# Two moves in a fused attention and gated-MLP kernel: half of the first query weights' loads to another engine's queue, two blocks of gate logits to an earlier stage

## The chip, the cores and the metric

The kernel runs on one core of a Trainium2 chip. The metric is the device time of one execution in microseconds (us), and a kernel's time is the median of several executions. A core has a matrix engine (TensorE, PE in the profile), a vector engine (VectorE, DVE), an engine for activations (ScalarE, ACT), GpSimd (POOL) and SyncE (SP), which here does nothing but issue DMA transfers. Every engine carries out its own instructions in a fixed order, and waits at an instruction until the semaphores that it names have been raised by other engines or by a transfer that has landed. Matrix products accumulate in PSUM, a small memory of eight banks of 128 x 512 fp32 elements; everything else lies in the on-chip SBUF (128 partitions) or in HBM.

## What is computed

The input x has S = 2048 rows of D = 1024 bf16 elements. Two branches are computed from it and are mixed by a gate for each row:

```python
g = _sigmoid((x * gate_w).sum(-1, keepdims=True))
# branch A: q, k, v = x @ wqkv, 32 heads of 32; each row attends to W = 8 rows,
# its own and those 2, 4, ... 14 rows before it; softmax; then @ wo
# branch B: gelu(x @ w_gate) * (x @ w_up) @ w_down, inner size 3584
return g * a + (1 - g) * b
```

## The kernel before

**Tiling.** The rows are handled in four chunks, c = 0 to 3, of 512 rows each, and two chunks form a pair. The weights stream through SBUF for each pair. All large products use a seven-product form of a 2 x 2 block product (Strassen's), so they need sums and differences of blocks, called forms here: of x (`x_forms`, lines L516 to L521, results T1 to T4), of the query, key and value weights (`qkv_forms`, L709), and of the down and output weights (`down_forms`, L1266). The forms are made on VectorE.

**Stages of a pair.** For each pair, `qkv_pair` computes queries, keys and values. Its first part, `first_pair`, begins with products of plain blocks (L592), whose weights need no forms, copies each finished bank to a second one as a start value (L602, L604), and goes on with products that need forms (L772; their results are read by L625, L637, L657, L667 and, for keys and values, L808 to L847). The `ffn` stage follows (L1136), with the gate and up products of branch B. `down` (L1305) multiplies by w_down and wo, and mixes the branches when banks are read (L1346, L1377, L1383): its `steps` are pairs (m, g), where m from 1 to 6 is one of the seven products and g a half of the chunk's rows. `main` (L1396) sets this order: chunks 0 and 1, then `down(0)`, then `qkv_pair(2)`, and so on.

**The gate.** `gate(c)` (L866) computes the logits x * gate_w of a chunk as products with the column of gate weights on TensorE (L874, eight matmuls for a chunk) into a bank; VectorE transposes the bank into a tile `zt` (L880), after which the bank is free, and copies 16 columns of it to `zq` (L884). `gate_sum` adds them up later (L898, L903). For chunks 0 and 1, `gate` is called inside `first_pair`; for 2 and 3, from `main` between the end of `down(0)` and `qkv_pair(2)`. The tile `zt` lies in one of two buffers with the tag `u2`; two other buffers have the tag `m5`. The down stage uses both tags as well.

**Attention.** Scores are made on VectorE: q times shifted k (L937) and sums over head parts (L943). The result is turned by a DMA transpose (L1006), softmaxed, spread by ScalarE (L1066), turned back by two DMA transposes (L1075), and multiplied with shifted v (L1084, 1.22 us each), which is summed (L1094, L1098, L1102). Every L1084 of a half chunk waits for the second L1075. All this work runs beside TensorE's stages, and the attention of chunk 1 is still going on when `down(0)` and `qkv_pair(2)` run.

**What sets the order.** A class `Weave` (L44) merges several streams of operations (`main`, `loads`, `x_forms`, `qkv_forms`, `attention`, `scores` and others) into one order for each engine. It always emits the operation with the smallest planned start plus a bias, where planned costs and due times are written into the code. Banks are handed out by `bank_take` to the earliest planned release. The chip then executes each engine's order as it stands. So moving one operation in `main` can reorder the others on VectorE and SyncE.

**Loads.** Nearly all loads are issued by SyncE in order, into 20 slots of a ring. At the start, SyncE issues two loads of query weights (L428, 512 KB each: blocks kt 0 to 1 and 2 to 3), a transposing load of half of chunk 0 (L357, in `early_x`), two more L428 (kt 4 to 5, 6 to 7), two L357 for chunk 1, and the key weights (L352). ScalarE issues one load of x rows (L312) and `gate_w` (L318), and then loads its activation table (L325). The other half of chunk 0 comes in as plain rows and is transposed by TensorE (L550), copied out by L559 and L561.

Of the kernel before, what the change touches and what calls it, by code (L numbers as in the profile page):

```python
# [11 lines left out]
F32 = mybir.dt.float32  # L12
AP = bass.AP

P = 128
# [4 lines left out]
SC = 512  # L20
# [134 lines left out]
def kernel(  # L155
# [12 lines left out]
    nc = tc.nc  # L168
    Bsz, S, D = A_x.shape
# [4 lines left out]
    KT = D // P  # L174
    KH = KT // 2
# [56 lines left out]
    n = NWIN * AC  # L232
# [83 lines left out]
    load_rows(nc.scalar, 2, 0)  # L316
    grow = xbuf[0:KT, 1, 0:P]
    nc.scalar.dma_start(out=grow, in_=gate_w.rearrange("(k p) -> k p", p=P))  # L318
    warm = xbuf[:, 0, 0:2]
    nc.vector.memset(warm, 0.0)  # L320
    for i, n_ in enumerate([SC] * 8):
# [15 lines left out]
    w.pipe = 3.2  # L337

    vbuf = hrow[:, 0:KT, :]
    qbuf = hrow[:, KT:2 * KT, :]  # L340
    NPREP = FH + NTH
    NSTG = 3
    def stage(i):
# [3 lines left out]
    def qkv_src(which, k0, n):  # L347
        return A_wqkv[k0 * P:(k0 + n) * P, which * D:(which + 1) * D].rearrange("(k p) n -> p k n", p=P)
# [75 lines left out]
    def loads():  # L424
        for kt in range(0, KT, 2):
            if kt == KH:
                yield from early_x(0)
            o = Op("SP", (2 * P * D * 2, 0.7), lambda kt=kt: nc.sync.dma_start(  # L428
                out=qbuf[:, kt:kt + 2], in_=qkv_src(0, kt, 2)), key=("wqkv", 0, 0, kt))
            yield o  # L430
            w.done["wqkv", 0, 0, kt + 1] = o
        yield from early_x(1)
        yield from load_qkv(0, 1)
        yield Op("SP", (KT * P * D * 2, 1.0), lambda: [nc.sync.dma_start(out=vbuf[:, hf * KH:(hf + 1) * KH],
                                                                        in_=qkv_src(2, hf * KH, KH)) for hf in range(2)],
                 key=("wqkv", 0, 2))
        yield load_prep(0)
        yield load_prep(2)
        yield from load_block(0, 0)
        yield load_prep(4)  # L440
        yield from load_block(0, 1)
        for b in range(2, NBLK):
            yield from load_block(0, b)
            if 4 + 2 * (b - 1) < NPREP:
                yield load_prep(4 + 2 * (b - 1))
        for sup in range(NSUP):
            c0 = 2 * sup
            more = sup + 1 < NSUP
            if more:
                yield from load_down(c0)  # L450
                for n in range(3):
                    yield from load_qkv(c0 + 2, QVK[n], range(KT) if n == 0 else [k for i in range(KH) for k in (i, i + KH)],
                                        [("wq", c0 + 2, QVK[n - 1], 3, KH - 1)] if n else [])
                for b in range(NE // FB):
                    yield from load_block(sup + 1, b, [("wq", c0 + 2, QVK[2], 3, KH - 1)])
                yield from load_down(c0 + 1)
                for b in range(NE // FB, NBLK):
                    yield from load_block(sup + 1, b)
            else:
                yield from load_down(c0)  # L460
                yield from load_down(c0 + 1)
# [404 lines left out]
    def gate(c):  # L866
        i, free = bank_take()
        dx = [("x", c, kt) for kt in range(KT)] if c else []

        def go():  # L870
            for r in range(KT // 4):
                for q in range(4):
                    kt = 4 * r + q
                    nc.tensor.matmul(banks[i][32 * q:32 * (q + 1), :], lhsT=gcol[:, kt:kt + 1].to_broadcast([P, 32]),  # L874
                                     rhs=xT(c, kt), start=(r == 0), stop=(r == KT // 4 - 1),
                                     tile_position=(0, 32 * q), skip_group_check=True)
        o = pe(KT // 4 + 1, go, ([free] if free else []) + dx + [("gcol",)], key=("z", c))
        yield o
        zt = work.tile([P, SC], F32, tag="u2", bufs=2, name="zt")
        e = dve(0.63, lambda: nc.vector.transpose(out=zt[:], in_=banks[i][:]), [o], bias=-2.0 if c < 2 else None)  # L880
        yield e
        bank_give(i, e)
        zq = small.tile([P, SC // 32], F32, tag="zq", bufs=2, name="zq")
        e = dve(0.1, lambda: nc.vector.tensor_copy(out=zq[:], in_=zt[:].rearrange("p (b j) -> p b j", j=32)[:, :, 0]), [e],  # L884
                key=("zq", c))
        yield e
        zc = small.tile([P, NST], F32, tag="zc", bufs=2, name="zc")
        ez = small.tile([P, NST], F32, tag="ez", bufs=2, name="ez")
        omg = small.tile([P, NST], F32, tag="omg", bufs=3, name="omg")
        gates[c] = (ez, omg, zq, zc)  # L890
# [439 lines left out]
    def down_rest(c, prod, ev, A, Bk, Dk, m5, u2, omg, steps):  # L1330
        s0 = c * SC
        last = c == NCH - 1
        eng = nc.sync if last else nc.gpsimd

        def evac(e_op, j, nh, ost):
            yield e_op
            yield Op("SP" if last else "POOL", (P * NW * 2, 0.5),
                     lambda: eng.dma_start(out=o2[s0 + j * P:s0 + (j + 1) * P, nh * NW:(nh + 1) * NW], in_=ost[0]),  # L1338
                     [e_op])

        def ost_tile(box):
            box.append(work.tile([P, 2 * SC], BF16, tag="gl", bufs=3, name="ost")[:, 0:NW])
            return box[0]

        def scaled(bk, om, dst):
            return nc.scalar.activation(out=dst, in_=banks[bk][:], func=ACT.Copy, scale=om)  # L1346

        for m, g in steps:
            if True:
                j1, j2 = 2 * g, 2 * g + 1  # L1350
                om1, om2 = omg[:, j1:j1 + 1], omg[:, j2:j2 + 1]
                box = []
                if m == 1:
                    o = yield from prod(A[g], m, g, False, [ev[g, "seed"]])
                    e = act(0.6, lambda g=g, om1=om1, box=box: scaled(A[g], om1, ost_tile(box)), [o, ("omg", c)])
                    yield from evac(e, j1, 0, box)
                    bank_give(A[g], e)
                elif m == 2:
                    Dk[g], fr = bank_take()
                    o = yield from prod(Dk[g], m, g, True, [fr])  # L1360

                    def cp(g=g, om2=om2):
                        m5[g] = work.tile([P, NW], F32, tag="m5", bufs=2, name="m5d")
                        scaled(Dk[g], om2, m5[g][:])
                    ev[g, "m5"] = act(0.6, cp, [o, ("omg", c)])
                    yield ev[g, "m5"]
                elif m == 3:
                    o = yield from prod(Bk[g], m, g, False, [ev[g, "seed"]])

                    def cp2(g=g, om1=om1):  # L1370
                        u2[g] = work.tile([P, NW], F32, tag="u2", bufs=2, name="u2d")
                        scaled(Bk[g], om1, u2[g][:])
                    ev[g, "u2"] = act(0.6, cp2, [o])
                    yield ev[g, "u2"]
                elif m == 4:
                    o = yield from prod(Bk[g], m, g, False, [ev[g, "u2"]])
                    ev[g, "x"] = dve(0.67, lambda g=g, om2=om2, box=box: nc.vector.scalar_tensor_tensor(  # L1377
                        out=ost_tile(box), in0=banks[Bk[g]][:], scalar=om2, in1=m5[g][:], op0=ALU.mult, op1=ALU.add),
                        [o, ev[g, "m5"]])
                    yield from evac(ev[g, "x"], j2, 1, box)  # L1380
                elif m == 5:
                    o = yield from prod(Dk[g], m, g, False, [ev[g, "m5"]])
                    e = dve(0.67, lambda g=g, om1=om1, box=box: nc.vector.scalar_tensor_tensor(  # L1383
                        out=ost_tile(box), in0=banks[Dk[g]][:], scalar=om1, in1=u2[g][:], op0=ALU.mult, op1=ALU.add),
                        [o, ev[g, "u2"]])
                    yield from evac(e, j1, 1, box)
                    bank_give(Dk[g], e)
                else:
                    o = yield from prod(Bk[g], m, g, False, [ev[g, "x"]])
                    e = act(0.6, lambda g=g, om2=om2, box=box: scaled(Bk[g], om2, ost_tile(box)), [o])  # L1390
                    yield from evac(e, j2, 0, box)
                    bank_give(Bk[g], e)
        if steps[-1][0] == 6:
            w.done[("down", c)] = o

    def main():  # L1396
# [8 lines left out]
        yield from ffn(0, 0, FT, parts)  # L1405
        yield from parts[2]
        yield from halo(2)
        yield from gate(2)
        yield from gate(3)
        yield from qkv_pair(2, [0])  # L1410
        yield from qkv_pair(2, [2, 1])
        yield from gate_sum(2)
# [43 lines left out]
```

## Time and profile before

Four executions took 725.27 to 726.68 us, with a median of 725.85.

| | before |
|---|---|
| median of 4 | 725.85 us |
| the profiled execution, its own time | 726.68 us |
| its span in the profile | 724.9 us |
| TensorE busy | 711.8 us (98%) |
| VectorE busy | 610.4 us (84%) |
| ScalarE busy | 323.9 us (45%) |
| GpSimd busy | 73.8 us (10%) |
| moved by DMA | 176.84 MB |

The profile is of one execution. Times in it count from the start of the span; an engine is busy while it carries out an instruction, and the time between two instructions of an engine is put down to whatever ended it: a semaphore of another engine, a transfer, or only its own issue. In the order of time, `qkv_pair(0)` begins at about 6 us, `down(0)` ends at 308.4 us and `qkv_pair(2)` follows it. A line number such as L880 is one of the program above.

### The profile page before, as it was taken

What the parts mean: (1) busy time and instruction counts of PE and PEld (TensorE: products, weight loads), DVE (VectorE), ACT (ScalarE), POOL (GpSimd) and SP (SyncE); (2) the same over time, 40 slices, a digit from 0 to 9 for tenths busy, and PEclk for the clock granted to TensorE, in tenths of its full rate; (3) what the DMA queues carried; (4) which work ended last, traced back from release to release, by engine and by line L of the source; (5) the groups of instructions that cost most, each with busy time, mean ns of one, the idle gap of its engine ahead of it and who ended that gap; (6) DMA issues with size and microseconds to landing.
All of it is one profiled execution on the core that took longest, in us unless ns stands there. A gap on an engine that the chain in (4) does not pass through costs nothing.

```text
span 724.9 us, 9885 instructions
## 1 busy us (share of the span) xinstructions
PE 711.8 (98%) x3337; PEld 343.1 (47%) x3337; DVE 610.4 (84%) x862; ACT 323.9 (45%) x547; POOL 73.8 (10%) x130
## 2 busy tenths in 40 slices
PE   7999999999999999979999999999999999999997
PEld 4556544444444444445655444444444444444443
DVE  4989999999999989799779998799999997849300
ACT  3354585555585522144465413257556755310110
POOL 0020333343121000100000000100000000001000
PEclk9999999999999999999999999999999999999999
DMA  9953899996897799932468899997657755999892
GB/s 255 365 193 95 251 293 312 368 312 213 184 264 217 244 231 339 345 127 81 148 181 283 263 316 329 321 318 188 176 152 183 181 155 165 304 308 375 295 335 96
DMA packets 184179, 176.84 MB, mean 244 GB/s; under 512 B 58304, under 2 KB 140224, under 8 KB 184000
## 3 DMA queue, kind: packets, MB, share of 16 engines
q1 hardware_dynamic: 174512, 145.53, 68.7%
q0 software_dynamic: 9328, 30.42, 11.6%
q8 instruction: 26, 0.43, 0.2%
q10 hardware_dynamic: 288, 0.26, 0.1%
q14 instruction: 25, 0.20, 0.1%
HBM read 132.12 MB, written 31.46 MB: 226 GB/s over the span
## 4 chain that ended last, share of the span: by engine, by line
PE 93%; DMA 3%; DVE 2%; SPq 1%; issue 0%; ACT 0%; DVEq 0%
PE ps L1136 47%; PE ps L1305 27%; PE ps L772 18%; DMA ring<-in_A_wqkv_dram 2%; DVE ring L709 1%; DMA ring<-dforms 1%; PE ps L592 1%; SPq L357 1%; DMA hT<-in_A_wqkv_dram 1%; DVE zt L880 0%; SPq L428 0%; DVE lend L520 0%; DVE tf L521 0%; DVE tf L518 0%; DVE lend L837 0%
## 5 line engine op out<-in xcount | busy, mean ns | idle before, releaser
L1136 PEld LDWEIGHTS <-ring 128*128 128x128 bf16 x1568 | 153.3, 98 | 185.0 <-issue 0.5
L1136 PE MATMUL ps<-lend,ring 128*128 128x512 bf16 x896 | 212.6, 379 | 0.0
L1136 PE MATMUL ps<-tf,ring 128*128 128x512 bf16 x672 | 164.3, 379 | 0.0
L1305 PE MATMUL ps<-ring,hT 128*128 128x512 bf16 x708 | 160.6, 379 | 0.0
L1305 PEld LDWEIGHTS <-hT 128*128 128x128 bf16 x708 | 69.3, 98 | 83.5
L1084 DVE TENSOR_TENSOR xbuf<-xbuf,lend 128x2048 bf16<-128x2048 bf16 x64 | 77.6, 1218 | 14.2 <-DMA xbuf<-xbuf 14.1
L772 PEld LDWEIGHTS <-ring 128*128 128x128 bf16 x512 | 64.8, 127 | 48.8 <-issue 2.5
L937 DVE TENSOR_TENSOR xbuf<-qo,lend 128x2048 bf16<-128x2048 bf16 x64 | 77.3, 1218 | 2.7 <-ACT lend L830 2.6
L943 DVE TENSOR_TENSOR xbuf<-xbuf 128x2048 bf16<-128x2048 bf16 x56 | 68.2, 1218 | 0.2
L772 PE MATMUL ps<-tf,ring 128*128 128x512 bf16 x256 | 58.4, 379 | 2.4 <-DVE tf L516 1.0
L772 PE MATMUL ps<-lend,ring 128*128 128x512 bf16 x256 | 57.9, 379 | 0.0
L1346 ACT ACTIVATE ost<-ps,omg 128x512 bf16<-128x512 f32 x16 | 11.0, 688 | 99.8 <-PE ps L1305 99.8
L1212 ACT ACTIVATE gl<-ps 128x512 bf16<-128x512 f32 x56 | 33.5, 598 | 48.3 <-PE ps L1136 47.2
L1168 ACT COPY ps<-ps 128x512 f32<-128x512 f32 x56 | 32.1, 573 | 50.9 <-PE ps L1136 50.6
L1305 PE MATMUL ps<-ring,qo 128*128 128x512 bf16 x192 | 49.3, 379 | 0.0
L1338 POOL DMA_DIRECT2D out_dram<-ost x24 | 13.0, 541 | 336.0 <-ACT ost L1346 248.3
L1185 DVE TENSOR_TENSOR hT<-hT,gl 128x1024 bf16<-128x1024 bf16 x56 | 38.4, 686 | 8.8 <-ACT hT L1178 8.7
L505 POOL DMA_DIRECT2D fforms<-ring x56 | 30.8, 551 | 144.0 <-DVE ring L496 137.9
L1224 DVE TENSOR_TENSOR u<-ps,u 128x512 f32<-128x512 f32 x56 | 38.4, 686 | 3.1 <-PE ps L1136 2.3
L1228 ACT ACTIVATE gl<-u 128x512 bf16<-128x512 f32 x56 | 35.4, 633 | 8.9 <-DVE u L1224 8.3
L1220 ACT COPY u<-ps 128x512 f32<-128x512 f32 x56 | 32.8, 586 | 14.6 <-PE ps L1136 14.6
L1094 DVE TENSOR_TENSOR xbuf<-xbuf 128x2048 bf16<-128x2048 bf16 x32 | 39.0, 1219 | 0.1
(120 smaller groups left out, 672.4 us busy)
## 6 DMA issues: line engine op xcount, KB each, us to landing
ring<-dforms SPq DMA_DIRECT2D x112, 256.0 KB, 5.0
ring<-in_B_w_down_dram SPq DMA_DIRECT2D x84, 256.0 KB, 5.3
ring<-in_B_w_gate_dram SPq DMA_DIRECT2D x56, 256.0 KB, 5.4
fforms<-ring POOLq DMA_DIRECT2D x56, 256.0 KB, 5.4
ring<-fforms SPq DMA_DIRECT2D x56, 256.0 KB, 4.0
ring<-in_B_w_up_dram SPq DMA_DIRECT2D x42, 256.0 KB, 4.6
ring<-in_A_wqkv_dram SPq DMA_DIRECT2D x32, 256.0 KB, 4.7
ring<-oforms SPq DMA_DIRECT2D x32, 256.0 KB, 5.7
```

Source lines behind the costliest of these rows:

```text
L772: nc.tensor.matmul(banks[bk][:], lhsT=lhsT, rhs=rhs[:, kt, :], start=(start and kt == 0), stop=(kt == KH - 1), skip_group_check=True)
L937: V(out=w3(box[t]), in0=q_b, in1=k_w, op=ALU.mult)
L943: V(out=w3(box[0]), in0=w3(box[0]), in1=w3(box[t]), op=ALU.add)
L1084: return dve(tt(n), taking(("p", t), lambda: V(out=w3(box["p", t]), in0=w3(box["ab"]), in1=v_w, op=ALU.mult)), [("qkv", c, 2, t), abo] + ( ...
L1094: V(out=p0.rearrange("p (u n) -> p u n", u=2), in0=lo, in1=hi, op=ALU.add)
L1136: nc.tensor.matmul(banks[bk][:], lhsT=wv[:, k, fl * P:(fl + 1) * P], rhs=rhs[:, k, :], start=(start and k == 0), stop=(k == KH - 1), skip_ ...
L1185: yield dve(tt(2 * SC), lambda hv=hv, gv=gv: nc.vector.tensor_tensor(out=hv, in0=hv, in1=gv, op=ALU.mult), [e, ev[f, "g1"], ev[f, "g2"]], ...
L1212: nc.scalar.activation(out=gl[f][:, r1 * SC:(r1 + 1) * SC], in_=banks[A[f]][:], func=ACT.Gelu_apprx_tanh)
L1220: nc.scalar.copy(out=u2[f][:], in_=banks[Bk[f]][:])
L1224: e = dve(tt(SC, True), lambda f=f: nc.vector.tensor_tensor(out=u2[f][:], in0=banks[Dk[f]][:], in1=u2[f][:], op=ALU.add), [o, ev[f, "u2"]])
L1228: ev[f, "g2"] = act(0.54, lambda f=f: nc.scalar.activation(out=gl[f][:, r2 * SC:(r2 + 1) * SC], in_=u2[f][:], func=ACT.Gelu_apprx_tanh), [ ...
L1305: nc.tensor.matmul(banks[bk][:], lhsT=l, rhs=wv[:, i, :], start=(start and k == 0), stop=(q == last and i == 1), skip_group_check=True)
```

## The change

Two independent things are changed.

First, the two loads of the query weights' blocks 4 to 5 and 6 to 7 are issued from ScalarE's queue, right after `gate_w`; SyncE's two issues of them between the transposing loads are gone. For the planner an empty operation is left in their place. Second, `gate(2)` and `gate(3)` are no longer called from `main` after `down(0)`, but within `down(0)`, ahead of its step (5, 0), and their `zt` takes a buffer with the tag `m5` in place of `u2`.

```diff
@@ load_rows, gate_w
     nc.scalar.dma_start(out=grow, in_=gate_w.rearrange("(k p) -> k p", p=P))
+    qbuf = hrow[:, KT:2 * KT, :]
+    for kt in (KH, KH + 2):
+        nc.scalar.dma_start(out=qbuf[:, kt:kt + 2], in_=A_wqkv[kt * P:(kt + 2) * P, 0:D].rearrange("(k p) n -> p k n", p=P))
     warm = xbuf[:, 0, 0:2]
...
-    qbuf = hrow[:, KT:2 * KT, :]
...
@@ loads
             if kt == KH:
                 yield from early_x(0)
-            o = Op("SP", (2 * P * D * 2, 0.7), lambda kt=kt: nc.sync.dma_start(
-                out=qbuf[:, kt:kt + 2], in_=qkv_src(0, kt, 2)), key=("wqkv", 0, 0, kt))
+            o = Op("SP", (2 * P * D * 2, 0.7 if kt < KH else 0.02), lambda kt=kt: nc.sync.dma_start(
+                out=qbuf[:, kt:kt + 2], in_=qkv_src(0, kt, 2)) if kt < KH else None, key=("wqkv", 0, 0, kt))
             yield o
@@ gate
-        zt = work.tile([P, SC], F32, tag="u2", bufs=2, name="zt")
+        zt = work.tile([P, SC], F32, tag="m5" if c > 1 else "u2", bufs=2, name="zt")
@@ down_rest
         for m, g in steps:
+            if (m, g) == (5, 0) and c == 0:
+                yield from gate(2)
+                yield from gate(3)
             if True:
@@ main
         yield from halo(2)
-        yield from gate(2)
-        yield from gate(3)
         yield from qkv_pair(2, [0])
```

In the order of the new program, TensorE's instructions differ only by the 16 gate matmuls, which stand before the 72 matmuls of the steps from (5, 0) on. On SyncE, the two L1075 of chunk 1's first half stand next to each other, ahead of the last six of eight loads of query weights for chunks 2 and 3. On VectorE, L520, L521, and the gates' L880 and L884 stand right after L1377 of step (4, 1), and part of the score work (L937, L943) moves behind them; two L1084 and one L1094 stand ahead of the eight L709 of the query weights.

## The prediction

> **What bounds the kernel now.** I read the busy shares first, to see which engine is full, then TensorE's waits, to see where it isn't.
>
> ```profile
> PE 711.8 (98%) x3337; PEld 343.1 (47%) x3337; DVE 610.4 (84%) x862; ACT 323.9 (45%) x547; POOL 73.8 (10%) x130
> ```
>
> TensorE is busy for 711.8 of 724.9 us, so only its 13 us of idle time and matmuls at a slow clock can be won. By the waits, one place holds the longest: 3.8 us before a block of L592, ended by VectorE's L880. The next are 1.6 (L592, for the first weights), 1.0 and 0.9 (L772), all before 22 us. The timeline round the longest wait (start, busy, engine, line; in brackets the idle time before and what ended it):
>
> ```profile
> 308.42 1.05 PE L874 MATMUL ps<-lend,gcol 128*32 128x512 bf16 x16
> ...
> 309.22 3.83 DVE L709 TENSOR_TENSOR ring<-ring 128x1024 bf16<-128x1024 bf16 x6 [6.09 <-DMA ring<-in_A_wqkv_dram]
> ...
> 309.40 2.81 PE L592 MATMUL ps<-lend,ring 128*128 128x512 bf16 x12
> ...
> 312.96 1.22 DVE L520 TENSOR_TENSOR lend<-lend 128x2048 bf16<-128x2048 bf16 x1
> 314.10 1.22 DVE L521 TENSOR_TENSOR tf<-lend,tf 128x2048 bf16<-128x2048 bf16 x1
> 315.23 0.71 DVE L880 STREAM_TRANSPOSE zt<-ps 128x512 f32<-128x512 f32 x1
> ...
> 315.99 5.87 PE L592 MATMUL ps<-lend,ring 128*128 128x512 bf16 x20 [3.79 <-DVE zt L880]
> ```
>
> The gate's matmuls are done at 309.47, but their PSUM bank comes free only when L880 has read it. On VectorE, L880 stands behind six Q forms (L709), which wait 6.09 us for weights, and behind L520 and L521. TensorE runs out of banks after 12 matmuls. The chain of waits says the same, backwards from the resumption:
>
> ```profile
> 303.24 5.76 DMA ring<-in_A_wqkv_dram
> ...
> 313.04 1.14 DVE lend L520
> 314.18 1.13 DVE tf L521
> 315.31 0.64 DVE zt L880
> 315.95 0.04 issue
> 315.99 5.87 PE ps L592 x20
> ```
>
> A second loss hides in the last line. Twenty matmuls take 5.87 us, against 20 x 0.216 = 4.32 at the usual spacing (32 in 7.07 at 328.61): the first seven start 0.43 apart. The table by stretches gives a clock of 0.87 here and 1.00 in the stretches on both sides:
>
> ```profile
> 308.40:322.00 13.60, 9.81 (x51) 5.28 (x51) 12.71 (x18) 5.18 (x11) 0.54 (x1) 0.87 0.36 109
> ```
>
> So this stage holds 3.79 + 1.55 = 5.3 us that a bank in time would save.
>
> The start of the kernel is the other place:
>
> ```profile
> 8.69 6.39 SPq L357 DMA_TRANSPOSE lend<-in_A_x_dram  x2
> 11.66 3.67 PE L592 MATMUL ps<-lend,hT 128*128 128x512 bf16 x16 [1.65 <-DMA hT<-in_A_wqkv_dram]
> 17.51 1.23 DVE L518 TENSOR_TENSOR tf<-lend,tf 128x2048 bf16<-128x2048 bf16 x1
> 21.30 1.02 PE L772 MATMUL ps<-tf,ring 128*128 128x512 bf16 x4 [0.94 <-DVE zt L880]
> ```
>
> TensorE waits 1.65 us for kt 4-5 (landed 11.62). What sets the resumption at 21.30 is VectorE's run from L518, which begins when the last transposed piece of x lands (17.41). DMA share from 5 to 22 us is 1.06: the engines are full.
>
> [...] 0.43 us spacing follows the 3.79 us gap, and the gap of 1.65 us has none. [...]
>
> **The gates, moved.** TensorE's work is the same, 16 matmuls in 1.05 us, now at 292.8, when (4,1) has been issued. Their rows of x are there: the last transposes of x are issued at 274.1 and land within 9.6 us; in the new program the gates' instructions carry no wait of their own, so no bank is late either. The down stage ends 1.05 later, at 309.4, and L592 follows without the 1.05: nothing won or lost.
>
> VectorE, walked with durations from its rows: L1377 of (4,1) ends at 293.7; L520 and L521 (1.14 each) end at 295.9; two L880 (0.64) and two L884 (0.1) end at 297.5. Both banks are free 12 us before L592 needs one. L592 runs 32 x 0.216 = 6.9 us: T1's products (L772) start at 316.4, not 321.70. Gain 5.3.
>
> What is late next: the score work that stood there (L937, L943, each 1.14) moves behind, so that the second attention transpose (L1075), in before at 303.77, is issued about 300 beside the first. By its rows it takes 3.3 to 7.1 us to land; I take 6, near the slow end, because two run side by side: 306. (The first alone landed at 304.7 in before, 6.1 after its issue.) On VectorE two L1084 and one L1094 now stand ahead of the Q forms: 306 + 3 x 1.14 = 309.4. The last Q weights land at 309 to 310 (309.00 in before, now behind both transposes on SP's queue). Eight forms x 0.62 end by 314.7; the first is ready at 310.3 and is needed at 316.4. The cover is 6 us.
>
> Then, in the order of the new program: 9 operations of 1.14, three L1098 (0.60), two L1102 (0.34), to 327.4, say 328 with gaps; four L657, four L667, eight L709 (0.60 each) to 337.1 (V forms; 339.88 in before); L1102 twice, L1094, L1098, two L937, two L943 = 7.0, to 344.1; then L837 (0.7) frees the V evacuation at 344.8. TensorE, 5.3 early, wants it at 349.33 - 5.3 = 344.0. New wait 0.8. Net gain of the stage 5.3 - 0.8 = 4.5. Every us that the landing is later than 306 costs one here. Behind this VectorE has over 6 us of idle between 350 and 371, so what is won stays won: TensorE runs on to 721 with one wait of 0.4.
>
> The `zt` tile's change of tag costs nothing: its buffers were last read by L1377 at 289.8 and 293.7, and L880 comes after.
>
> **The weight loads, moved.** SP loses two issues (1.08 us from 7.56), so the next transpose can be issued at about 7.5 instead of 8.69. ScalarE issues two more, ahead of its table load (1.28) and exponential, which by its first issues (0.49, 0.64) then end at 4.6 instead of 3.42; the loads wait for nothing, since nothing has used their buffer. Its first real work is L559 at 5.21: cover 0.6 us. Bytes are the same and the engines full, so bandwidth gives only the gaps in the DMA's work, 0.5 to 0.6 us by the DMA shares of 0.63 in 9 to 10 and 0.87 in 14 to 15 us. The four weight loads land by about 10; the first transpose[...] slips from 9.53 to 11.6-12.5, so TensorE's second half of L592 starts at 12.05 instead of 11.66; but the last transpose lands about 16.4 to 16.9 instead of 17.41 and L518 starts at 16.95 instead of 17.51. TensorE resumes at 20.75: gain 0.55. If the first transpose slips further, it is a loss of 0.7; if every gap goes, a gain of 0.9. I take 0.3.
>
> **Sum.** 4.5 + 0.3 = 4.8 against the profiled execution's 726.68 (span 724.9 and 1.8 around it): 721.9. That execution is the slowest of the four, 0.83 over the median of 725.85; so on the median 721.05, say 721.1.
>
> **Rivals.** (1) VectorE becomes the bound of the Q and V stage: attention's transposes land near 308, L837 is 2.8 late, and only 2.5 + 0.3 is kept: 723.0. For it: VectorE is 93% busy from 308.4 to 322 and 26.01 of 28.00 us after. Against: SP issues both early. (2) Everything is won, 5.3 + 0.9: 719.6. It needs landings near 305[...]. (3) Slower: the two L1084 and the L1094 ahead of the Q forms wait for a late L1075. The gain is 4.5 less the landing's delay over 306, and is used up at 310.8; at 313, the stage loses 2.2: 727.8 with the start's 0.3. Against it: the landing would take 13 us, where the slowest in before took 7.1. (4) The change does not do it: the bank is free but Q's forms miss TensorE, because their weights wait for ring slots or SP; the idle time moves from 312 to 316. For forms at 321.5 as before, weights would have to land at 316: about 725.5.
>
> **How the numbers follow.** My case 0.62 (719.9 to 722.4), VectorE bound 0.20, all won 0.06, not done 0.05, slower 0.07. From no change, 0.2% (1.45 us) can be told; faster is 0.62 + 0.20 + 0.06 = 0.88, less 0.01 for rival 1's tail; the same 0.05 + 0.01 = 0.06; slower 0.07. Of the start, both ends (-0.7, +0.9) lie within my case's own width. The range takes in nearly all of my case, most of rival 1 (721.9 to 724.2, with its landing at 307 to 309.3) and half of rival 2: 719.6 to 723.8.
>
> **What would show it.** Right: no wait of L592 for L880 near 312, clock 1.00 from 308 to 322, first T1 product near 316.4, VectorE waiting for transposed attention weights until about 306, a new wait of L772 for L837 of about 0.8 near 344, and TensorE's resumption at 20.8. Wrong: L1084 waiting beyond 308, a wait of L772 for L709 near 316, L559 later than 5.21, or the first transposed x landing after 13.

## The result, and the profile after

The changed kernel takes 724.02 us (median of 43 executions, 721.58 to 728.22), the kernel before 725.8 (64 executions). The ratio is 0.9976, with a 95% interval of 0.9967 to 0.9985: faster, by 1.8 us where 4.7 had been forecast, and outside the range (719.6 to 723.8).

The profiled execution of after took 722.18 us with a span of 720.4. That is 4.5 us below the profiled execution of before, so the two profiles, laid side by side, seem to confirm the forecast of 4.8. Line numbers in a view are those of the program that ran: in after most lines stand two later than in the program above (L594, L774, L839, L876 and L882 there are L592, L772, L837, L874 and L880), in the experiments up to a dozen. The busy time of after's page:

```profile
PE 710.4 (99%) x3337; PEld 343.3 (48%) x3337; DVE 610.2 (85%) x862; ACT 324.0 (45%) x547; POOL 73.8 (10%) x130
```

The stage that the gates had held up, in the timeline of after (start, busy, engine, line; in brackets the idle time before and what ended it):

```profile
292.70 1.05 PE L876 MATMUL ps<-lend,gcol 128*32 128x512 bf16 x16
...
295.76 0.71 DVE L882 STREAM_TRANSPOSE zt<-ps 128x512 f32<-128x512 f32 x1
...
304.16 2.36 DVE L1086 TENSOR_TENSOR xbuf<-xbuf,lend 128x2048 bf16<-128x2048 bf16 x2 [1.75 <-DMA xbuf<-xbuf]
...
309.23 7.07 PE L594 MATMUL ps<-lend,ring 128*128 128x512 bf16 x32
...
309.50 5.52 DVE L711 TENSOR_TENSOR ring<-ring 128x1024 bf16<-128x1024 bf16 x8 [1.72 <-DMA ring<-in_A_wqkv_dram]
...
316.14 6.21 PE L774 MATMUL ps<-tf,ring 128*128 128x512 bf16 x28
```

L594's 32 matmuls run in one piece, 0.216 us apart, and T1's products begin at 316.14 (forecast: 316.4; before: 321.70). The table by stretches has the same stretch as before at full clock, with TensorE busy throughout:

```profile
308.40:322.00 13.60, 13.60 (x65) 8.07 (x64) 12.21 (x16) 9.01 (x17) 0.54 (x1) 1.00 0.47 155
```

What is left stands in TensorE's waits. The second of them is the new one:

```profile
PE ps L594 <- DMA lend<-in_A_x_dram: 1.8, 1, 1.8
PE ps L774 <- DVE lend L839: 1.8, 1, 1.8
PE ps L774 <- DVE zt L882: 1.1, 1, 1.1
```

It comes from score work that stands ahead of the V evacuation (L839) on VectorE, again in the timeline:

```profile
340.27 2.35 DVE L939 TENSOR_TENSOR xbuf<-qo,lend 128x2048 bf16<-128x2048 bf16 x2
342.54 2.48 DVE L945 TENSOR_TENSOR xbuf<-xbuf 128x2048 bf16<-128x2048 bf16 x2
344.94 1.28 DVE L839 TENSOR_TENSOR lend<-ps,m5q 128x512 bf16<-128x512 f32 x2
...
345.68 1.89 PE L774 MATMUL ps<-tf,ring 128*128 128x512 bf16 x8 [1.75 <-DVE lend L839]
```

At the start, the first block of L594 has a wait as long as before, but it is now ended by the first transposed piece of x, which lands at 12.29 instead of 9.53, and no longer by weights (those of kt 4 to 7 land at 9.15 and 10.71). TensorE resumes after the gate of chunk 1 at 21.13, against 21.30:

```profile
7.02 3.61 PE L594 MATMUL ps<-lend,hT 128*128 128x512 bf16 x16 [0.67 <-ACT lend L561]
...
12.42 3.65 PE L594 MATMUL ps<-lend,hT 128*128 128x512 bf16 x16 [1.79 <-DMA lend<-in_A_x_dram]
...
21.13 1.24 PE L774 MATMUL ps<-tf,ring 128*128 128x512 bf16 x5 [1.14 <-DVE zt L882]
```

So the pair of profiles fits the forecast, while the medians give less than half of it. The granted clock of every execution, which is recorded with its time, shows why a pair of profiles can mislead here:

| kernel | executions | mean us | clock 0.999 or more: number, median | below 0.999: number, median |
|---|---|---|---|---|
| before (beside the experiments, and e1) | 157 | 725.25 | 72, 723.9 | 85, 726.1 |
| after (with e2) | 64 | 723.71 | 38, 722.5 | 26, 724.8 |

The profile of before (clock 0.998) is of the right group, that of after (1.000) of the left one. Which execution was profiled is chance, so that the pair fits the forecast is luck. Like with like, the change saves 1.3 us, and after still has executions in which the clock falls, although the place where before lost it is gone. With two groups a median jumps from one to the other (after's two measurements gave 724.02 and 722.96), so means are compared below where shares matter.

### The profile page after: what moved, and what is told of

The parts are those of the page before. It is cut to its first block, busy times and chain, and to the rows that moved or that the text cites. A ratio compares the mean times of both kernels' runs of the same rounds, so it can differ in the third digit from the quotient of the medians.

```text
span 720.4 us, 9893 instructions
## 1 busy us (share of the span) xinstructions
PE 710.4 (99%) x3337; PEld 343.3 (48%) x3337; DVE 610.2 (85%) x862; ACT 324.0 (45%) x547; POOL 73.8 (10%) x130
## 4 chain that ended last, share of the span: by engine, by line
PE 97%; DMA 1%; DVE 1%; issue 0%; SPq 0%; ACT 0%; DVEq 0%
PE ps L1138 47%; PE ps L1307 30%; PE ps L774 18%; PE ps L594 1%; DMA lend<-in_A_x_dram 1%; PE ps L876 0%; DVE ring L711 0%; SPq L430 0%; DVE tf L520 0%; DVE lend L839 0%; DVE zt L882 0%; ACT ost L1348 0%; DVE hT L711 0%; PE ps L900 0%; SPq L312 0%
## 5 line engine op out<-in xcount | busy, mean ns | idle before, releaser
L774 PEld LDWEIGHTS <-ring 128*128 128x128 bf16 x512 | 64.7, 127 | 49.1 <-issue 4.2
L774 PE MATMUL ps<-tf,ring 128*128 128x512 bf16 x256 | 58.4, 379 | 2.9 <-DVE lend L839 1.8
L774 PE MATMUL ps<-lend,ring 128*128 128x512 bf16 x256 | 57.9, 379 | 0.0
L1226 DVE TENSOR_TENSOR u<-ps,u 128x512 f32<-128x512 f32 x56 | 38.5, 687 | 2.6 <-PE ps L1138 2.3
```

The source lines that it names most:

```text
L774: nc.tensor.matmul(banks[bk][:], lhsT=lhsT, rhs=rhs[:, kt, :], start=(start and kt == 0), stop=(kt == KH - 1), skip_group_check=True)
L1226: e = dve(tt(SC, True), lambda f=f: nc.vector.tensor_tensor(out=u2[f][:], in0=banks[Dk[f]][:], in1=u2[f][:], op=ALU.add), [o, ev[f, "u2"]])
```

## Experiments

**Theory C (clock).** A gap in TensorE's work lowers the granted clock in some executions, for some eight matmuls (in the profile of before to 0.50, from 315.44 to 318.85 us). The moved gates remove one such gap; the moved loads make another. **Rival G (gap).** The two groups of times come from the length of gaps, and the loads are harmless; what the gates' gain lost is VectorE's lateness.

**e1, e2: second profiles of both kernels,** unchanged.

> The kernel before, unchanged, for a second profile. Its executions lie in two groups, near 723.6 and near 726.1 us, and the profile of before (726.68, clock 0.998) is of the upper one, that of after (722.18, clock 1.000) of the lower. Theory C (clock): the groups differ by seven matmuls at half clock behind a gap of TensorE. If this profile is of the lower group (clock 1.000), the gap of about 3.8 us near 312 is there but the matmuls after it stand 0.216 us apart; if of the upper, 0.43. Rival G (gap): the groups differ by the length of the gap at 312 (by 2 us or more), as the query weights land at different times.

> The changed kernel, unchanged, for a second profile. Theory C: in the upper group (about 724.6, clock 0.998) seven or more matmuls at 0.43 us spacing follow one of the remaining gaps: the 1.8 us near 12 or the 1.75 us near 345; in the lower group (722.2) none do. Rival G: no slow matmuls in either, and the gap near 345 is 2 us longer in the upper.

e1 measured 724.98 us (12 executions; ratio 0.9996, 0.9976 to 1.0016). Its profile is of an execution of 724.08 us at a clock of 1.000. In the timeline, the wait at 312 is there but shorter, and nothing behind it is slow:

```profile
309.21 2.81 PE L592 MATMUL ps<-lend,ring 128*128 128x512 bf16 x12
...
314.76 4.48 PE L592 MATMUL ps<-lend,ring 128*128 128x512 bf16 x20 [2.74 <-DVE zt L880]
```

Twenty matmuls in 4.48 us, where the profile of before had 5.87 after a wait of 3.79. Both theories have a part: the waits differ by 1.05 and the slow matmuls by 1.4, together 2.4, about the distance of the groups. e2 measured 722.96 (20 executions, 7 of them below 0.999; ratio 0.998, 0.9965 to 0.9995). Its profile, at 1.000, shows no slow matmul behind waits of 2.04 (first block of L594) and 2.60 us (L774 for L839). The V evacuation's wait thus varies from 1.75 to 2.60. No profile of the changed kernel with a fallen clock was obtained.

**e3, e4: each part of the change alone.**

```diff
# e3_loads_only, against after: the gates back in main, their tile back to tag "u2"
-            if (m, g) == (5, 0) and c == 0:
-                yield from gate(2)
-                yield from gate(3)
# e4_gates_only, against after: the two loads back on SyncE
-    for kt in (KH, KH + 2):
-        nc.scalar.dma_start(out=qbuf[:, kt:kt + 2], in_=A_wqkv[...])
```

> Only the two weight loads go to ScalarE's queue; the gates stay behind the down stage. My step said a gain of 0.3 (-0.7 to +0.9): 725.5 against 725.8. By the traces (TensorE resumes at 21.13 instead of 21.30) 0.2. The stage at 308 to 322 should be as in before, with the gap of 3.8 us for the gate's bank. Rival: the first block of L592 starting at 7.02 instead of 6.40, and a longer wait behind it, cost 0.5 or more, or bring a slow clock at the start: 726.5.

> Only the gates move into the down stage; the loads stay on SyncE. My step said a gain of 4.5: 721.3. By the trace of after, 5.3 less 1.75 for the new wait for the V evacuation near 345, plus 0.4 for one that is gone: 3.9, 721.9. By the medians of before and after, if this part carries the whole change, 1.8: 724.0. The gap near 312 should be gone and one of 1.5 to 1.8 us stand near 345.

e3 measured 726.52 (22 executions; 1.0013, 0.9999 to 1.0027), 1.0 above the 725.48 of before on the same chip, and by the means 1.3 (726.59, 725.30). The interval just includes no change; what is clear is the clock: 20 of 22 executions lie below 0.999, where before has 40 of 67. Its profile (clock 0.995) shows the price, in TensorE's timeline:

```profile
6.04 1.92 PE L594 MATMUL ps<-lend,hT 128*128 128x512 bf16 x8 [0.67 <-ACT lend L561]
9.34 1.95 PE L594 MATMUL ps<-lend,hT 128*128 128x512 bf16 x8 [1.38 <-DMA hT<-in_A_wqkv_dram]
13.31 5.33 PE L594 MATMUL ps<-lend,hT 128*128 128x512 bf16 x16 [2.03 <-DMA lend<-in_A_x_dram]
```

The weights of kt 2 to 3 land at 9.29 instead of 7.67 and split the first half; then the first transposed piece of x, at 13.18, delays the second. Between 7.96 and 13.31 TensorE works 1.95 us. The 16 matmuls behind take 5.33 us, where 3.65 is usual: 1.7 us, in matmuls about 0.43 apart from 14.0 to 17.4. The stretch from 11 to 20 us has a clock of 0.81 in its table, against 1.00 in both kernels' first profiles:

```profile
11.00:20.00 9.00, 6.97 (x30) 2.90 (x28) 5.84 (x10) 2.61 (x5) 0.00 (x0) 0.81 1.14 277
```

e4 measured 722.91 (22 executions; 0.9972, 0.9961 to 0.9984), between the 721.9 that the traces and the 724.0 that the medians had suggested, with 2 of 22 executions below 0.999, against 26 of 64 with the loads moved as well. Its waits, the two longest in sum:

```profile
PE ps L772 <- DVE lend L837: 1.9, 2, 1.7
PE ps L592 <- DMA hT<-in_A_wqkv_dram: 1.5, 1, 1.5
```

By the means, the gates alone save 2.2 (725.30 to 723.13), and with the loads 0.6 of it is lost again (723.71). The intervals of e4 and of the whole change overlap, so that 0.6 is not certain by the times alone.

**e5, e6: the gaps filled, the waits left.** Matmuls with zeros for weights (`zz`, a column that GpSimd clears once at the start) add nothing to a bank that they go to, but keep TensorE at work. They are additional work, none is left out.

```diff
+        def fill(t, n):
+            def go():
+                for _ in range(n):
+                    nc.tensor.matmul(banks[A[t]][:], lhsT=zz[:, 0:1].to_broadcast([P, P]), rhs=xT(ca, 0),
+                                     start=False, stop=True, skip_group_check=True)
+            return Op("PE", 0.0, go, [fr[t]])
# e5_after_filled, in after
         if not c:
+            yield fill(0, 8)
             for t in ts:
                 yield mm(t, [KH, KH + 1])
# e6_before_filled, in before
             if c:
+                if t == 3:
+                    yield fill(0, 12)
                 A[t], fr[t] = bank_take()
```

> The changed kernel, and eight matmuls of zeros that add nothing to a bank stand between the two halves of the first block of L594, where TensorE otherwise waits 1.8 to 2.0 us for the first transposed piece of x. Theory C: the loads' price is the half clock that this wait brings in part of the executions; kept busy, TensorE keeps its clock, nearly every execution is at a clock of 0.999 or more, and the median is 722.5, as of the changed kernel's executions at full clock, against 724.0 of all. Rival: the clock falls elsewhere (behind the wait near 345), or the eight matmuls (1.7 us) only add to the path: the median stays at 723.5 to 725.

> The kernel before, and twelve matmuls of zeros (2.6 us) that add nothing to a bank stand ahead of the product of L592 that waits for the gate's bank near 312. Theory C: the wait stays (2.7 to 3.8 us from the last useful matmul), but no matmul after it is slow; the executions at a lower clock become rare and the median falls from 725.5 to 723.7 to 724.2. That part of what the moved gates save is clock, the rest the wait. Rival: the two groups come from the length of the wait alone, and the median stays at 725.5.

e5 measured 722.56 (22 executions, one below 0.999; 0.9966, 0.9955 to 0.9977). The timeline of e5's TensorE, in which L593 is the fill:

```profile
8.97 1.95 PE L603 MATMUL ps<-lend,hT 128*128 128x512 bf16 x8 [0.58 <-DMA hT<-in_A_wqkv_dram]
10.76 1.89 PE L593 MATMUL ps<-lend,wj 128*128 128x512 bf16 x8
12.93 3.61 PE L603 MATMUL ps<-lend,hT 128*128 128x512 bf16 x15 [0.29 <-DMA lend<-in_A_x_dram]
```

The transposed piece comes as late as in e3 (12.89), but of what follows 15 matmuls take 3.61 us, and the clock is 1.00 from 11 to 20 us. By the means, useless work makes the changed kernel 1.0 us faster (723.71 to 722.75), and it does so by taking away the executions below 0.999; those at full clock stay where they were (722.5 in both). e6 measured 723.86 (14 executions, none below 0.999; 0.9988, 0.9976 to 1.0): exactly before's own executions at full clock (723.9 on that chip), 1.4 under its median of 725.27. The interval of the ratio reaches 1.0, but the means differ clearly too (725.15 to 723.92), and no execution of e6 lies in the lower group, against 23 of 51 of before. So the groups of before go with the clock, and of what the gates save, 1.4 us by the medians (1.2 by the means) is clock. Theory C holds in both places; G's part is the variation of the waits within it.

**e7: the V evacuation ahead of the score sums,** in e4's kernel.

```diff
-out=out_, in0=banks[Bk[t]][:], in1=m5[t][:], op=ALU.add), [o, ev["m5", t]], key=key)
+out=out_, in0=banks[Bk[t]][:], in1=m5[t][:], op=ALU.add), [o, ev["m5", t]], key=key,
+    bias=-1.5 if c and which == 2 and not g else None)
# and the same at L847
```

> The gates moved, the loads on SyncE, and the V evacuations (L837, L847) put ahead of score sums that stand before them on VectorE. Near 345 TensorE waits 1.7 us for L837 with the gates alone. If that wait is what the gates' gain lost, it goes and the median is 721.2 against 722.9; if VectorE is full in this stage, the work pushed back makes the next evacuations or the attention's transposes late, and the median is 722.5 to 724.

Measured: 723.53 (20 executions; 0.9981, 0.997 to 0.9993). The wait near 345 is gone, but TensorE pays near 471 in the feed-forward stage. There ScalarE, which has to free the bank, stands idle for 3.30 us until VectorE has done an L1226 that has its place among the attention's products. The waits of e7:

```profile
PE ps L1138 <- ACT m L1196: 2.0, 2, 1.8
...
PE ps L772 <- DVE lend L837: 0.2, 1, 0.2
```

The wait was moved, not removed. Six of 20 executions are below 0.999.

**e8: the weight loads ahead of the transposes, all on SyncE,** in before.

```diff
         for kt in range(0, KT, 2):
-            if kt == KH:
-                yield from early_x(0)
...
+        yield from early_x(0)
         yield from early_x(1)
```

> The kernel before, with all four weight loads ahead of the first transposing load of x on SyncE's queue; nothing on ScalarE's. If the loads' price comes from the order of bytes (the first transposed piece lands later, TensorE waits longer in front of the second half of L592), this shows it more strongly: the wait 2.5 us or more instead of 0.7 to 1.7, ended by the transposed x, slow matmuls behind it, median 726.5 to 727.5 against 725.5. If it comes from a second queue, the time is as before, 725 to 726.

Measured: 739.94 (4 executions; 1.0202, 1.0172 to 1.0231). This time says nothing of the loads, for much of it comes from other waits:

```profile
PE ps L771 <- DVE qo L656: 7.9, 1, 7.9
PE ps L591 <- DVE zt L879: 3.5, 1, 3.5
PE ps L591 <- DMA lend<-in_A_x_dram: 3.2, 1, 3.2
```

The first, near 41 us, follows a stretch of 12.80 us in which VectorE stands idle before its weight forms (L708), until a load has landed at 38.8; how the edit brings that about isn't shown. But its first 17 us answer the question. With no load on ScalarE's queue, the transposed pieces of x land at 12.91, 14.86 and 16.70 and the weights of kt 4 to 7 at 9.18 and 10.54; in after it was 12.29, 14.41, 16.39, and 9.15, 10.71. The wait for x was 3.25 us, with matmuls 0.43 apart behind it. So in these runs the late landing (12.91 and 12.29, against 9.53 in before) comes from what is fetched before what, whichever queue does it.

**A wait's length or its place: the kept traces.** The second wait of e8's list is longer than those that had slow matmuls behind them in e3 (2.03 us and 3.08, the latter between 308 and 322 us, a stretch with a clock of 0.88), and yet nothing behind it is slow. In e8's timeline:

```profile
319.85 2.81 PE L591 MATMUL ps<-lend,ring 128*128 128x512 bf16 x11
326.18 4.05 PE L591 MATMUL ps<-lend,ring 128*128 128x512 bf16 x18 [3.52 <-DVE zt L879]
```

So length alone doesn't decide. The trace of before records when the granted clock changed: it rose at 4.83 us, fell to 0.50 at 315.44 and was back at 1.00 at 318.85, 3.41 us later. From the rise to the fall it is 310.61 us, 91 x 3.413. In e3 the clock was at 0.50 from 14.01 to 17.42, again 3.41 us. The tables by stretches, cut into steps of that length counted from the changes of each profile's clock, show what comes before a fall. The number after the first comma is TensorE's work in the step, and the third from the end is the clock. First before, then e3, then e1, then e8 with its 3.52 us wait, which lies across two steps:

```profile
312.03:315.44 3.41, 0.18 (x1) 0.00 (x0) 3.41 (x5) 0.57 (x1) 0.00 (x0) 1.00 0.00 0
315.44:318.86 3.42, 2.87 (x7) 1.13 (x7) 3.42 (x7) 0.57 (x1) 0.00 (x0) 0.50 0.01 2
...
10.60:14.01 3.41, 1.38 (x8) 0.68 (x7) 3.25 (x6) 0.57 (x1) 0.00 (x0) 1.00 1.28 264
14.01:17.42 3.41, 3.41 (x10) 1.35 (x9) 2.31 (x3) 0.23 (x1) 0.00 (x0) 0.50 1.13 260
...
310.59:314.00 3.41, 1.43 (x7) 0.83 (x6) 3.41 (x5) 1.45 (x3) 0.00 (x0) 1.00 0.07 23
314.00:317.41 3.41, 2.65 (x13) 1.77 (x13) 3.41 (x8) 1.16 (x2) 0.00 (x0) 1.00 0.00 0
...
321.13:324.55 3.42, 1.48 (x7) 0.86 (x6) 3.31 (x5) 1.55 (x3) 0.00 (x0) 1.00 0.11 40
324.55:327.96 3.41, 1.78 (x9) 1.20 (x9) 3.41 (x7) 0.46 (x1) 0.00 (x0) 1.00 0.00 0
```

In these tables a step with 0.18 us of work (before) and one with 1.38 (e3) were followed by one at half clock, steps with 1.43 (e1) and 1.48 (e8) by one at full clock. That the work in a step is what counts is the author's reading of these few, and no run tests it. If it holds, it would also explain why one program has two groups of times: whether a wait of 2 to 4 us empties a step would depend on where the steps fall.

**e9 to e12: another place for the gates, and combinations.** The walk through VectorE's order shows it idle for 1.75 us before 304.16 and 1.72 us before 309.50, while score work that had been ahead of the gates waits until 340. With the gates two steps later, that work stays ahead of them.

```diff
# e9_gates_60: e4 with
-            if (m, g) == (5, 0) and c == 0:
+            if (m, g) == (6, 0) and c == 0:
# e10_gates_filled: e4 with fill(0, 4) at the start
# e11_gates_60_filled: e9 with fill(0, 4) at the start
# e12_after_60_filled: e5 with the gates at (6, 0)
```

> The gates moved ahead of step (6, 0) instead of (5, 0), the loads on SyncE. Four score operations (L937, L943) then stay ahead of the gates on VectorE, where it otherwise waits for transposed attention weights, and no longer stand in front of the V evacuations near 345. If the 1.7 us wait for the V evacuation is what the gates' gain lost, it shrinks below 0.5 and the median is 721.3 to 721.8 against 722.9 of the gates at (5, 0). If VectorE's load in this stage is the bound wherever the gates stand, the wait turns up elsewhere and the median stays at 722.7 to 723.5.

> The gates at (5, 0), the loads on SyncE, and four matmuls of zeros (0.86 us) between the two halves of the first block of L592. Against the changed kernel with its wait filled (722.56 in the run before), it prices the loads alone with the clock held: by the traces the loads save 0.2 to 0.3, so 722.8 here. If the loads' gain at full clock is nothing, 722.5.

> The gates at (6, 0), the loads on SyncE, four matmuls of zeros at the start. By the sum of the two parts: e9 less 0.1 to 0.3 for the executions in which the clock fell: 721.2.

> Both parts of the change, with the gates at (6, 0) and eight matmuls of zeros at the start. By the sum: 721.0, the fastest of all; 722.5 if the place of the gates makes no difference.

| run | median us | executions | ratio to before (95%) | below 0.999 |
|---|---|---|---|---|
| e9 | 721.22 | 6 | 0.9945 (0.9925 to 0.9964) | 0 |
| e10 | 722.45 | 22 | 0.9964 (0.9953 to 0.9975) | 1 |
| e11 | 721.42 | 6 | 0.9949 (0.9929 to 0.9969) | 0 |
| e12 | 721.24 | 6 | 0.9946 (0.9924 to 0.9967) | 0 |

e9 beats both kernels: 4.0 us under before's median and 2.5 under after's mean. In its waits, the V evacuation near 345 no longer appears; the 0.4 is the old one near 370:

```profile
PE ps L592 <- DMA hT<-in_A_wqkv_dram: 1.2, 1, 1.2
PE ps L772 <- DVE zt L880: 1.2, 1, 1.2
...
PE ps L772 <- DVE lend L837: 0.4, 1, 0.4
```

On VectorE, the gates still come 7 us ahead of the bank's need at about 312, and the Q forms start at 307.46 (in e9's timeline):

```profile
303.04 1.22 DVE L521 TENSOR_TENSOR tf<-lend,tf 128x2048 bf16<-128x2048 bf16 x1
304.18 0.71 DVE L880 STREAM_TRANSPOSE zt<-ps 128x512 f32<-128x512 f32 x1
...
307.46 0.69 DVE L709 TENSOR_TENSOR ring<-ring 128x1024 bf16<-128x1024 bf16 x1 [1.74 <-DMA ring<-in_A_wqkv_dram]
```

e10 against e5 (722.45 and 722.56) prices the loads with the clock held: nothing that can be measured (on two chips, on which before took 725.26 and 725.27). e11 and e12 add nothing to e9, whose own first wait (1.2 us, for weights) doesn't take the clock in its six executions.

## Why the prediction failed, by its steps

**Right.** The place and the mechanism of the gates: the bank in time, L592 without a break, T1's products at 316.14 (316.4), Q forms starting at 309.50 (309.4), V forms ending at 337.6 (337.1), L880's wait gone. VectorE was not held up by the turned attention weights: they were there at 304.16, 2 us earlier than worked out, so rival 3 is excluded. The start of the Q forms was set by their weights alone (forecast to land at 309 to 310): VectorE had been free for 1.7 us, where the forecast had it busy until 309.4. The sign of the whole was right. (Rival 3's sum counts the start's 0.3 twice: from a gain of 4.5, a landing at 313 makes the stage lose 2.5, and 728.05 comes out instead of 727.8. Nothing rests on it.)

**Wrong: "Sum", the step from one execution to the median.** The 4.8 was worked out against a profile with the 3.79 us wait and the slow matmuls behind it, and was then subtracted in full from the median. But only part of the executions of before has that loss (40 of 67 below a clock of 0.999), and with the clock kept the wait was 2.74 in e1. The terms measure: clock 1.2 to 1.4 (e6, means and medians), and wait 2.74 + 0.40 in e1 less 1.70 + 0.16 in e4, 1.3; together 2.5 to 2.7, where e4 saved 2.2 to 2.6. The 1.3 rests on one profile of each; by the executions at full clock alone it is 0.9 (723.8 to 722.9 in the mean). The spread of the four times shown, 725.27 to 726.68, was taken for noise. As an estimate from these figures, of the 3 us that are missing this step accounts for about 1.3 (5.3 forecast, 1.2 to 1.4 and 2.74 found), the next for some 0.7, and the loads for 0.9.

**Mis-sized: the new wait for L837.** Forecast 0.8, measured 1.75 (after), 1.70 (e4), 2.60 (e2). The walk had the right order and lost 0.5 us by 337.6 and about 0.3 more by L839. The 0.5 is a slip in its sum: 328 and sixteen operations of 0.60 make 337.6, where it has 337.1. Since every lateness there is TensorE's, it is the term with the least margin. That it comes from this order and isn't VectorE's limit, e9 shows: 1.7 us less by another place.

**Wrong in sign: "The weight loads, moved".** Forecast: 0.3 gained, between -0.7 and +0.9. Measured by means: 1.3 lost alone (e3), 0.6 lost beside the gates (e4 to after). At full clock the 0.3 is even there (722.5 in after, 722.8 in e4), though e10 against e5 gives none; the share of executions below full clock, 26 of 64 against 2 of 22, outweighs it. The landings, the author's estimate, came out nearly right (first transposed piece 11.6 to 12.5 forecast, 12.29 in after, but 13.18 in e3; last 16.39; resumption 20.75 forecast, 21.13 found). Two things were missed. ScalarE's loads also delay SyncE's second load (kt 2 to 3, from 7.67 to 8.41 in after and 9.29 in e3), so that e3 has two waits. And the waits were priced at their length, because before's 1.65 us had no slow matmuls behind it; but behind 0.4 us more (2.03 in e3) the clock was at 0.50 for 3.41 us. Nor does a wait's length alone tell its price: half clock followed one of 3.08 us (e3, between 308 and 322), and none followed one of 3.52 (e8), of 2.60 (e2) or of 2.74 (e1). Taking the 1.65 us that had cost no clock in one profile for the mark of a harmless wait was the error. The second queue itself was not shown to gain anything: in e8, with all four weight loads on one queue, the weights of kt 4 to 7 land at 9.18 and 10.54, in after at 9.15 and 10.71, and e10 against e5 (722.45 and 722.56) shows no gain from the issue time.

**Open.** No profile shows the changed kernel itself with a fallen clock; that it falls behind the first block of L594 follows from e3's profile and e5's effect, but isn't seen directly. That the work in a step of 3.41 us decides whether the clock falls is the author's reading of the four profiles above, not tested.

## What to carry to other kernels

When times of one kernel lie in two groups, find out first which group the profile is of, and price the change against each; a saving read from one execution must not be taken off the median of all. In these runs a wait on TensorE cost its length, and behind some waits the clock was at 0.50 for 3.41 us as well: behind one of 2.03 us it was, behind one of 3.52 it wasn't. So a change that lengthens a wait by less than half a us (here from 1.65 to 2.03) can lose more than that (1.7 us in the matmuls behind it in e3), in part of the executions. Filling the wait with useless matmuls is a cheap test (e5 and e6: 1 of 36 executions below a clock of 0.999). When work is moved ahead on a full engine, look at what it pushes back: here the saving went from 2.6 to 4.0 us once that work stayed where the engine had been idle.

## What was not expected of the hardware

Twelve matmuls that compute nothing make the kernel before 1.4 us faster (725.27 to 723.86; 1.2 by the means), and eight make the changed one 1.0 us faster by the mean (723.71 to 722.75). Two loads of 512 KB on a second queue delayed a transposing load by 2.8 us (9.53 to 12.29), nearly as much as the same loads ahead of it on its own queue (12.91). A wait of 3.52 us left the clock at full (e8), while one of 2.03 was followed by half of it (e3).
